# Attention logits with the head indicator stationary and the products streaming through four 32-column tiles

## The chip, the cores and the metric

The kernel runs on one core of a Trainium2 chip. The metric is the device time of one execution in microseconds (us). In the profile PE is TensorE (its matmuls), PEld its weight loads, DVE is VectorE, ACT is ScalarE, POOL is GpSimd.

## The reference

One transformer block over 2048 positions of width 576: a modulated layer norm, local attention with 32 heads of 18 channels, a projection, a second modulated layer norm, and a gated MLP with 4608 hidden channels. The change touches the logits of the attention alone. Each position looks at eight keys, at distances 0, 2, ... 14:

```python
idx = pos[:, None] - off[None, :]            # off = 0, 2, ..., 14
kg = k[:, :, idx_c, :].reshape(B, H, S, W, Dh)      # W = 8, Dh = 18
logits = jnp.einsum('bhsd,bhswd->bhsw', q, kg) * scale
logits = jnp.where(mask[None, None, :, :], logits, -1000000000.0)
attn = _softmax(logits, axis=-1)
```

## The kernel before

The sequence is cut into 8 chunks of 256 positions. Three pieces of work run per chunk: `stage_a` (layer norm, the q, k and v projections `pq` and `pv`), `stage_b` (logits, softmax, weighted sum of V, output projection `pw`, second layer norm) and `mlp` (matmuls `pgu`, `acc`, `accr`). `stage_a` and `stage_b` of later chunks are generators that the MLP loop advances one `yield` at a time, so that their matmuls mix with those of the MLP. Before the first MLP there is a start-up in which `stage_b(0)` and `stage_a(1)` alternate.

The logits before: for each of the eight key offsets, DVE multiplies q by the shifted k (`prod`, channels on the partitions). TensorE then sums each head's 18 channels, with `prod` as the stationary operand and a 0/1 head indicator `ind` of 32 columns streaming.

```python
lnp   = tile_pool(name="lnp", bufs=2)    # ln_xn
hTp   = tile_pool(name="hTp", bufs=3)    # ln_hT
prodp = tile_pool(name="prodp", bufs=2)
smp   = tile_pool(name="smp", bufs=2)    # dd
# ... (stage_b)
lg = psum_tile([P, ST, W, H], F32, name="lg")
for i in range(W):
    off = HALO - DIL * (W - 1 - i)
    prod = prodp.tile([P, KT, CH], BF, name="prod")
    nc.vector.tensor_tensor(prod[:], qT[:], kT[:, :, off:off + CH], ALU.mult)
    with hp():
        for j in range(ST):                # two halves of 128 positions
            for m in range(KT):            # five slices of 128 channels
                nc.tensor.matmul(lg[:, j, i, :], lhsT=prod[:, m, j * P:(j + 1) * P], rhs=ind[:, m, :],
                                 start=(m == 0), stop=(m == KT - 1))
    if i % 2 == 1:
        yield
# ... softmax over lg: maskneg (chunk 0 alone), mx, dd, ssum, attn

def interleave(g1, g2):                    # advances stage_b and stage_a in turn
    gs = [g for g in (g1, g2) if g is not None]
    while gs:
        for g in list(gs):
            try:
                next(g)
                yield
            # ...
```

Of the kernel before, what the change touches and what calls it, by code (L numbers as in the profile page):

```python
# [7 lines left out]
BF = mybir.dt.bfloat16  # L8
F32 = mybir.dt.float32
ALU = mybir.AluOpType  # L10
# [5 lines left out]
P = 128  # L16
D = 576
DP = 640
KT = 5
H = 32  # L20
DH = 18
W = 8
DIL = 2
FF = 4608
FT = FF // P
HALO = 16
EPS = 1e-5
NEG = -1.0e9
CH = 256
ST = CH // P  # L30
# [26 lines left out]
def kernel(  # L57
# [14 lines left out]
    nc = tc.nc  # L72
# [6 lines left out]
    def hp():  # L79
        return tc.high_priority() if cfg["hi_pe"] else nullcontext()  # L80
# [2 lines left out]
    wts = ctx.enter_context(tc.tile_pool(name="wts", bufs=1))  # L83
    dramp = ctx.enter_context(tc.tile_pool(name="dramp", bufs=1, space=DRAM))
    xin = ctx.enter_context(tc.tile_pool(name="xin", bufs=6))
    lnp = ctx.enter_context(tc.tile_pool(name="lnp", bufs=2))
    small = ctx.enter_context(tc.tile_pool(name="small", bufs=2))
    hTp = ctx.enter_context(tc.tile_pool(name="hTp", bufs=3))
    qkp = ctx.enter_context(tc.tile_pool(name="qkp", bufs=2))
    vstage = ctx.enter_context(tc.tile_pool(name="vstage", bufs=2))  # L90
    prodp = ctx.enter_context(tc.tile_pool(name="prodp", bufs=2))
    smp = ctx.enter_context(tc.tile_pool(name="smp", bufs=2))
    attnp = ctx.enter_context(tc.tile_pool(name="attnp", bufs=2))
    vshp = ctx.enter_context(tc.tile_pool(name="vshp", bufs=2))
    ps_att = ctx.enter_context(tc.tile_pool(name="ps_att", bufs=3, space=PSUM))
# [7 lines left out]
    def psum_tile(shape, dt, name):  # L103
        return ps_att.tile(shape, dt, name=name, tag="att")

    ident = consts.tile([P, P], BF, name="ident")
# [3 lines left out]
    ind = consts.tile([P, KT, H], BF, name="ind")  # L110
# [252 lines left out]
    def stage_b(ci):  # L363
        s0 = ci * CH
        cd = chunk[ci]
        x_t, qT, kT = cd["x_t"], cd["qT"], cd["kT"]
        vshs = []
        for j in range(ST):
# [2 lines left out]
            src = bass.AP(vd.tensor, vd.offset + base * D, [[D, P], [DIL * D, W], [1, D]])  # L371
            dma_vsh.dma_start(vsh[:].rearrange("p w d h -> p w (d h)"), src)
            vshs.append(vsh)
        lg = psum_tile([P, ST, W, H], F32, name="lg")
        for i in range(W):
            off = HALO - DIL * (W - 1 - i)
            prod = prodp.tile([P, KT, CH], BF, name="prod")
            nc.vector.tensor_tensor(prod[:], qT[:], kT[:, :, off:off + CH], ALU.mult)  # L378
            with hp():
                for j in range(ST):  # L380
                    for m in range(KT):
                        nc.tensor.matmul(lg[:, j, i, :], lhsT=prod[:, m, j * P:(j + 1) * P], rhs=ind[:, m, :],  # L382
                                         start=(m == 0), stop=(m == KT - 1))
            if i % 2 == 1:
                yield
        mx = small.tile([P, ST, H], F32, name="mx")
        dd = smp.tile([P, ST, W, H], F32, name="dd")
        if ci == 0:
# [42 lines left out]
        for j in range(ST):  # L431
            pw = psum_tile([P, 512], F32, name="pw")
            with hp():
                for m in range(KT):
                    nc.tensor.matmul(pw[:], lhsT=oT[:, m, j * P:(j + 1) * P], rhs=wo[:, m, 0:512],  # L435
                                     start=(m == 0), stop=(m == KT - 1))
                for m in range(KT):
                    nc.tensor.matmul(pwr[:, j, :], lhsT=oT[:, m, j * P:(j + 1) * P], rhs=wo[:, m, 512:D],
                                     start=(m == 0 and j == 0), stop=(m == KT - 1), skip_group_check=True)
# [93 lines left out]

    run(stage_a(0))
    run(interleave(stage_b(0), stage_a(1) if NCH > 1 else None))
    for ci in range(NCH):
        gb_ = stage_b(ci + 1) if ci + 1 < NCH else None
        ga_ = stage_a(ci + 2) if ci + 2 < NCH else None
        bg = interleave(gb_, ga_)
        mlp(ci, bg)  # L540
        run(bg)
# [30 lines left out]
```

## Time and profile before

| | before |
|---|---|
| time, median of 4 runs | 650.53 us (649.53 to 653.12) |
| PE busy | 92% of the span |
| PE busy from 45 to 75 us | 21.4 of 30 us, clock 0.76 |
| first MLP matmul | 68.8 us |
| end of the first MLP | 160.0 us |
| one chunk after that | 75.0 us |

From the page of the kernel before, busy time per engine, and two rows of the 40 slices (tenths busy; granted clock in tenths):

```profile
PE 597.5 (92%) x5700; PEld 450.0 (70%) x5788; DVE 319.9 (49%) x733; ACT 277.0 (43%) x518; POOL 141.1 (22%) x221
...
PE   2766999999999999999999999999999999999996
...
PEclk9979799999999999999999999999999999999999
```

TensorE is full from the fifth slice on. Only the first 70 us or so have room. Busy time in two stretches, in the order PE, PEld, DVE, ACT, POOL, then clock, DMA share and GB/s, first for the end of the start-up, then for one chunk:

```profile
45.00:75.00 30.00, 21.38 (x215) 14.55 (x217) 22.23 (x43) 13.28 (x28) 6.91 (x14) 0.76 0.83 255
```
```profile
310.03:385.05 75.02, 72.97 (x696) 55.12 (x706) 38.80 (x90) 34.13 (x64) 16.52 (x26) 1.00 0.38 116
```

The waits of PE in that chunk (who waited for whom, us in total, times, longest) come to 1.3 us:

```profile
PE oT_pA L425 <- DVE o_sb L416: 0.7, 1, 0.7
PE ln_pA L287 <- ACT ln_xn L278: 0.4, 1, 0.4
PE lg L382 <- DVE prod L378: 0.2, 1, 0.2
```

The group of the logit matmuls (count, busy us, mean ns of one, idle before):

```profile
L382 PE MATMUL lg<-ind,prod 128*128 128x32 bf16 x640 | 32.4, 180 | 2.3 <-DVE prod L378 2.1
```

The 180 ns is the length of one record, not what one matmul costs. The PE timeline of the kernel before, in which neighbours of one group are merged (start us, length us, count at the end), shows the pace:

```profile
319.53 0.22 PE L287 MATMUL ln_pB<-ident,ln_xn 128*128 128x128 bf16 x1
319.58 0.66 PE L382 MATMUL lg<-ind,prod 128*128 128x32 bf16 x20
320.09 0.19 PE L471 MATMUL accr<-wd_blk,hh 128*128 128x64 bf16 x1
...
321.17 0.18 PE L382 MATMUL lg<-ind,prod 128*128 128x32 bf16 x1
321.19 0.22 PE L287 MATMUL ln_pA<-ident,ln_xn 128*128 128x128 bf16 x1
321.25 0.18 PE L382 MATMUL lg<-ind,prod 128*128 128x32 bf16 x1
```

Twenty logit matmuls take 0.51 us from 319.58 to the next start at 320.09: 25 ns each, and 80 of them 2.0 us a chunk. This is the floor for small matmuls that the Trainium skill gives ("TensorE: Matmul & The Clock Gate", "Back-to-back issue gap": about 25 ns for 1 to 64 columns). At the 109 ns that 256 columns take here, 32 columns alone would need about 14 ns (an estimate), so a form with longer streams could save at most some 1 us of 75 us. The last lines show that logit matmuls and layer norm transposes alternate freely, at no cost.

### The profile page before, as it was taken

To read this page: it belongs to the slowest core of one execution; us is meant where nothing else is said; L and a number is where in the kernel's file an instruction comes from. 1 tells how busy PE (TensorE), PEld (TensorE's weight loads), DVE (VectorE), ACT (ScalarE), POOL (GpSimd) and SP (SyncE) were. 2 spreads that over 40 slices of the span, in tenths; PEclk is the share of its full clock that TensorE was granted. 3 is DMA by queue.
4 is the path that set the end of the run, shared out by engine and by line. 5 is a ranking of instruction groups with operands and counts; after the bars stand their busy time and mean duration, and the time that the engine had idled before them with its cause. 6 is when DMAs were issued, how large, how long until landed. Compare 5 with 4: busy or idle time off the path is not lost.

```text
span 647.4 us, 13700 instructions
## 1 busy us (share of the span) xinstructions
PE 597.5 (92%) x5700; PEld 450.0 (70%) x5788; DVE 319.9 (49%) x733; ACT 277.0 (43%) x518; POOL 141.1 (22%) x221
## 2 busy tenths in 40 slices
PE   2766999999999999999999999999999999999996
PEld 1543767677767777677776777677776777777774
DVE  5387788712891158611893138811594152113112
ACT  2523646433653337433563337433443335333332
POOL 7014021222112221322212221112211222222220
PEclk9979799999999999999999999999999999999999
DMA  8699658693326341533406332353322333333331
GB/s 254 173 315 286 195 181 257 204 284 101 95 60 216 97 127 55 189 105 92 129 29 230 92 104 69 113 175 93 110 74 57 96 110 89 92 96 111 97 99 41
DMA packets 41094, 87.24 MB, mean 135 GB/s; under 512 B 4857, under 2 KB 27721, under 8 KB 41033
## 3 DMA queue, kind: packets, MB, share of 16 engines
q0 software_dynamic: 15872, 61.35, 31.7%
q1 hardware_dynamic: 22857, 22.66, 11.9%
q10 hardware_dynamic: 2304, 2.36, 1.1%
q8 instruction: 45, 0.74, 0.5%
q14 instruction: 16, 0.13, 0.1%
HBM read 81.62 MB, written 5.40 MB: 134 GB/s over the span
## 4 chain that ended last, share of the span: by engine, by line
PE 63%; DVE 22%; ACT 7%; DMA 4%; issue 1%; SPq 1%; POOL 0%; ACTq 0%
PE pgu L482 30%; PE pgu L484 8%; DVE vsh L412 5%; PE accr L471 4%; PE pw L435 3%; DVE vsh L414 3%; DVE ln_stats L267 2%; ACT ln_xn L278 2%; ACT ln_hT L296 2%; DMA wgu<-in_B_w_up_dram 2%; PE ln_pA L287 1%; PE lg L382 1%; DVE hh L494 1%; ACT gu L493 1%; PE acc_8289 L469 1%
## 5 line engine op out<-in xcount | busy, mean ns | idle before, releaser
L482 PE MATMUL pgu<-ln_hT,wgu 128*128 128x256 bf16 x2304 | 337.2, 273 | 0.0
L493 ACT CAST gu<-pgu 128x512 bf16<-128x512 f32 x288 | 168.6, 586 | 263.4 <-PE pgu L484 263.2
L482 PEld LDWEIGHTS <-wgu 128*128 128x128 bf16 x2304 | 205.5, 98 | 50.8 <-issue 1.2
L494 DVE TENSOR_TENSOR hh<-gu 128x256 bf16<-128x256 bf16 x288 | 83.5, 291 | 284.5 <-ACT gu L493 284.1
L477 POOL DMA_DIRECT2D wd_blk<-in_B_w_down_dram x144 | 102.5, 712 | 343.3 <-PE accr L471 337.8
L471 PE MATMUL accr<-wd_blk,hh 128*128 128x64 bf16 x576 | 110.9, 193 | 3.8
L469 PEld LDWEIGHTS <-hh 128*128 128x128 bf16 x576 | 56.3, 98 | 40.9 <-DVE hh L494 4.1
L484 PE MATMUL pgu<-ln_hT,wgur 128*128 128x256 bf16 x288 | 78.6, 273 | 0.0
L484 PE MATMUL pgu<-ln_hTu,wgur 128*128 128x256 bf16 x288 | 78.5, 272 | 0.0
L336 PE MATMUL pq<-ln_hT,wqk 128*128 128x256 bf16 x400 | 56.9, 279 | 8.1 <-ACT ln_hT L296 6.3
L484 PEld LDWEIGHTS <-wgur 128*128 128x128 bf16 x576 | 56.4, 98 | 6.3
L471 PEld LDWEIGHTS <-hh 128*128 128x128 bf16 x576 | 56.2, 98 | 3.0
L378 DVE TENSOR_TENSOR prod<-qT,kT 128x1280 bf16<-128x1280 bf16 x64 | 51.1, 821 | 12.9 <-ACT kT L341 9.9
L336 PEld LDWEIGHTS <-wqk 128*128 128x128 bf16 x400 | 38.4, 100 | 16.4 <-issue 7.0
L412 DVE TENSOR_TENSOR vsh<-vsh,attn 128x4608 bf16<-128x4608 bf16 x16 | 40.3, 2555 | 0.2
L382 PE MATMUL lg<-ind,prod 128*128 128x32 bf16 x640 | 32.4, 180 | 2.3 <-DVE prod L378 2.1
L382 PEld LDWEIGHTS <-prod 128*128 128x128 bf16 x640 | 26.9, 98 | 9.9 <-DVE prod L378 7.5
L296 ACT ACTIVATE ln_hT<-ln_pA,modc 128x256 bf16<-128x256 bf16 x32 | 18.1, 564 | 18.0 <-PE ln_pA L287 8.3
L287 PE MATMUL ln_pA<-ident,ln_xn 128*128 128x128 bf16 x128 | 16.5, 232 | 8.7 <-ACT ln_xn L278 7.9
L287 PEld LDWEIGHTS <-ln_xn 128*128 128x128 bf16 x160 | 13.2, 103 | 15.0 <-ACT ln_xn L278 13.5
L351 PE MATMUL pv<-wv,ln_hT 128*128 128x512 bf16 x72 | 21.0, 378 | 1.0 <-ACT kT L341 0.5
L414 DVE TENSOR_TENSOR vsh<-vsh 128x2304 bf16<-128x2304 bf16 x16 | 21.4, 1369 | 0.0
(218 smaller groups left out, 581.7 us busy)
## 6 DMA issues: line engine op xcount, KB each, us to landing
wd_blk<-in_B_w_down_dram POOLq DMA_DIRECT2D x144, 288.0 KB, 3.3
vsh<-vd POOLq DMA_DIRECT2D x16, 1152.0 KB, 7.4
wgu<-in_B_w_gate_dram SPq DMA_DIRECT2D x9, 512.0 KB, 6.7
wgu<-in_B_w_up_dram SPq DMA_DIRECT2D x9, 512.0 KB, 7.6
wm<-in_w_mod_dram SPq DMA_DIRECT2D x6, 576.0 KB, 5.6
x_t<-in_A_x_dram SPq DMA_DIRECT2D x16, 144.0 KB, 2.8
vd<-v_sb ACTq DMA_DIRECT2D x16, 144.0 KB, 1.8
out_dram<-o_t SPq DMA_DIRECT2D x16, 144.0 KB, 3.1
```

The source lines that it names most:

```text
L336: nc.tensor.matmul(pq[:, gi, :], lhsT=wqk[:, kt, t, m * P:(m + 1) * P], rhs=hT[:, kt, :], start=(kt == 0), stop=(kt == KT - 1))
L378: nc.vector.tensor_tensor(prod[:], qT[:], kT[:, :, off:off + CH], ALU.mult)
L382: nc.tensor.matmul(lg[:, j, i, :], lhsT=prod[:, m, j * P:(j + 1) * P], rhs=ind[:, m, :], start=(m == 0), stop=(m == KT - 1))
L412: nc.vector.tensor_tensor(vsh[:], vsh[:], attn[:, j, :, None, :].to_broadcast([P, W, DH, H]), ALU.mult)
L414: ge.tensor_tensor(vsh[:, 0:4], vsh[:, 0:4], vsh[:, 4:8], ALU.add)
L469: nc.tensor.matmul(acc[j][:], lhsT=hh[:, j * P:(j + 1) * P], rhs=wd_blk[:, f % WDB, 0:512], start=(f == 0), stop=(f == FT - 1))
L471: nc.tensor.matmul(accr[:, j, :], lhsT=hh[:, j * P:(j + 1) * P], rhs=wd_blk[:, f % WDB, 512:D], start=(f == 0 and j == 0), stop=(f == FT - ...
L477: dma_wd.dma_start(wd_blk[:], B_w_down[f * P:(f + WDB) * P, :].rearrange("(k p) n -> p k n", p=P))
L482: nc.tensor.matmul(pgu[:, t, :], lhsT=wgu[:, kt, t, f * P:(f + 1) * P], rhs=h2T[:, kt, :], start=(kt == 0), stop=False)
L484: nc.tensor.matmul(pgu[:, t, :], lhsT=wgur[:, f * P:(f + 1) * P], rhs=(h2T[:, KT - 1, :] if t == 0 else h2Tu[:]), start=False, stop=True)
L493: nc.scalar.copy(gu[:], pgu[:])
L494: hh_inst = nc.vector.tensor_tensor(hh[:], gu[:, 0, :], gu[:, 1, :], ALU.mult)
```

## The change

The operands swap roles: the indicator (32 columns) becomes stationary and the product streams, 256 positions at once. A 32-column weight has a quarter of the usual 128 columns, so four key offsets go to four column tiles (a quarter of the array's columns each), whose outputs land on PSUM partitions 0, 32, 64 and 96. The result has heads and offsets on the partitions, so ACT evicts it as bf16 and four transposes bring positions back to the partitions. A group needs four products at a time: `prod` gets five buffers, and three other pools shrink to make room.

```diff
-    lnp = ctx.enter_context(tc.tile_pool(name="lnp", bufs=2))
+    lnp = ctx.enter_context(tc.tile_pool(name="lnp", bufs=1))
-    hTp = ctx.enter_context(tc.tile_pool(name="hTp", bufs=3))
+    hTp = ctx.enter_context(tc.tile_pool(name="hTp", bufs=2))
-    prodp = ctx.enter_context(tc.tile_pool(name="prodp", bufs=2))
-    smp = ctx.enter_context(tc.tile_pool(name="smp", bufs=2))
+    prodp = ctx.enter_context(tc.tile_pool(name="prodp", bufs=5))
+    smp = ctx.enter_context(tc.tile_pool(name="smp", bufs=1))
# ... the loop of the old form goes, and in its place:
+        WG = W // 2
+        lgT = psum_tile([P, 2, CH], F32, name="lgT")
+        for g in range(2):
+            prods = []
+            for i in range(g * WG, (g + 1) * WG):
+                off = HALO - DIL * (W - 1 - i)
+                prod = prodp.tile([P, KT, CH], BF, name="prod")
+                nc.vector.tensor_tensor(prod[:], qT[:], kT[:, :, off:off + CH], ALU.mult)
+                prods.append(prod)
+                if i % 2 == 1:
+                    yield
             with hp():
+                for m in range(KT):
+                    for wi in range(WG):
+                        nc.tensor.matmul(lgT[wi * H:(wi + 1) * H, g, :], lhsT=ind[:, m, :], rhs=prods[wi][:, m, :],
+                                         start=(m == 0), stop=(m == KT - 1), skip_group_check=True)
+            yield
+        lgs = smp.tile([P, 2, CH], BF, name="lgs")
+        nc.scalar.copy(lgs[:], lgT[:])
+        lg = psum_tile([P, ST, W, H], BF, name="lg")
+        with hp():
+            for j in range(ST):
+                for g in range(2):
+                    nc.tensor.transpose(lg[:, j, g * WG:(g + 1) * WG, :].rearrange("p w h -> p (w h)"),
+                                        lgs[:, g, j * P:(j + 1) * P], ident[:])
+        yield
```

More of the change, by code (lines that the diff above doesn't have):

```diff
@@ L373, in stage_b @@
             vshs.append(vsh)
-        lg = psum_tile([P, ST, W, H], F32, name="lg")
-        for i in range(W):
-            off = HALO - DIL * (W - 1 - i)
-            prod = prodp.tile([P, KT, CH], BF, name="prod")
-            nc.vector.tensor_tensor(prod[:], qT[:], kT[:, :, off:off + CH], ALU.mult)
-            with hp():
-                for j in range(ST):
-                    for m in range(KT):
-                        nc.tensor.matmul(lg[:, j, i, :], lhsT=prod[:, m, j * P:(j + 1) * P], rhs=ind[:, m, :],
-                                         start=(m == 0), stop=(m == KT - 1))
-            if i % 2 == 1:
-                yield
+        WG = W // 2
[9 more added lines that the diff above has]
+                    yield
+            with hp():
+                for m in range(KT):
[12 more added lines that the diff above has]
+        yield
         mx = small.tile([P, ST, H], F32, name="mx")
```

## The prediction

> **What bounds the kernel now.** TensorE. The page's busy table has PE 92%, DVE 49%, ACT 43%. Between 145 and 425 us the table by stretches has PE at 68.0 of every 70 us, clock 1.00, and one chunk lasts 75.0 us (the `o_t` evictions in the chain of waits stand at 235.0, 310.0, 385.1). In the PE timeline matmuls follow each other at stream pace: 109 ns per 256-column matmul, 216 ns per 512-column one. The waits of PE for anybody in the chunk 310 to 385 sum to only 1.3 us. So time moves only with TensorE's stream time per chunk, or with the first 75 us, where PE is busy for 45 us and latency counts.
>
> **What is removed.** 80 matmuls per chunk `lg<-ind,prod` (128x32), 640 in all. The groups list shows 32.4 us busy, 180 ns each, but that overlaps: in the PE timeline 20 of them start within 0.50 us, so 25 ns each. Their true cost is 2.0 us per chunk, 16 us in all, plus about 0.3 us of waits for `prod` per chunk.
>
> **What is added, per chunk.**
> - 40 matmuls of 256 columns, weights of 32 columns. One after the other they would cost 40 x 109 ns = 4.4 us. If four 32-column tiles stream at once (the Trainium skill, "TensorEngine Tiling (Array Packing)", Key Properties, says that tiles operate independently; no run here shows it yet), 10 x about 115 ns = 1.15 us. I expect mostly overlap: 1.2 to 1.5 us.
> - 4 transposes, about 56 ns each in the timeline: 0.22 us.
> - Mode switches. The same section says that a change of tiling mode drains the array. A matmul's record outlasts its own 13 ns stream by about 160 ns, so I estimate 0.15 us a switch. At least four per chunk (0.6 us). The order of `lg` and `ln_pA` before alternates one by one at 321 and 326 us; if the new matmuls get interleaved with full-width ones like that, 8 to 12 switches (1.2 to 1.8 us).
> - ACT: one 128x512 eviction, 0.59 us (as `gu`). ACT has room. DVE reads bf16 logits: no change expected. `prod` stays 0.82 us x8, but with five buffers no longer waits for PE.
>
> **Sum.** Before 2.0 + 0.3 us; after 1.3 + 0.22 + 0.6 to 1.5 us. Per chunk -0.2 to +0.7 us, in all -2 to +6 us.
>
> **Other parts.** In the start-up, the longer way from `prod` to softmax (eviction 0.6 us, transposes, two handovers) adds about 1 us for chunk 0. One buffer for `ln_xn`, two for `ln_hT`: an `hT` for a later chunk must wait until the running MLP has read its `hT`; background work moves later, into the next MLP, but PE has matmuls to fill with, so I expect little (0 to +2 us). The `x1` buffers already hold background work back to the end of each MLP (`x1` follows `o_t` directly at 311.9 us).
>
> **Prediction.** 652 us; 643 to 672 us should hold it 8 times in 10. Faster by over 2%: 0.04; within 2%: 0.77; slower by over 2%: 0.19.
>
> **What would show the steps.** Right: `lgT` matmuls start about 25 to 35 ns apart in the PE timeline, in blocks of 20; gaps of 0.1 to 0.2 us at each border between `lgT` and full-width matmuls; the chunk stays within 1 us of 75.0; PE waits stay small.
>
> **What would make it wrong.** If `lgT` matmuls start 109 ns apart, the tiles don't overlap, and the time is about 670 us. If switches cost nothing, about 645 us. If PE waits for `ln_hT` or the `att` PSUM buffers near MLP borders, the smaller pools cost more than I think, and the first 75 us or the `o_t` spacing will show it.

## More of the kernel before

The build fixes the order of each engine's instructions ahead of time. It starts from the order in the program, lets `hp()` (high priority) come forward, and passes over what it believes is not ready. Where a `yield` stands therefore decides what comes first.

## The result

The changed kernel takes 668.32 us (median of 4 runs, 665.76 to 668.65), against 650.53 us before. The ratio is 1.0265, 95% interval 1.0237 to 1.0293: slower by 2.7%.

| | before | after |
|---|---|---|
| time | 650.53 us | 668.32 us |
| logit matmuls | 640 of 32 columns | 320 of 256 columns, 32 transposes |
| PE busy from 45 to 75 us | 21.4 us | 13.8 us |
| chunk 0's softmax starts | 37.5 us | 44.9 us |
| first MLP matmul | 68.8 us | 77.2 us |
| end of the first MLP | 160.0 us | 160.7 us |
| one chunk after that | 75.0 us | 76.3 us |
| longer chunk in which the last background work lands | none | 79.5 us |

Both end the first MLP at nearly the same time, but the kernel before had by then done more: 200 of 400 `pq` matmuls, against 154. The deferred work lands later.

From the page after, busy time and the group of the new matmuls:

```profile
PE 611.4 (92%) x5500; PEld 443.6 (67%) x5500; DVE 319.6 (48%) x733; ACT 279.9 (42%) x526; POOL 145.1 (22%) x221
...
L388 PE MATMUL lgT<-prod,ind 128*32 128x256 bf16 x320 | 21.5, 287 | 0.8 <-DVE prod L381 0.8
```

The PE timeline after, one chunk's logits in the steady part:

```profile
351.46 0.61 PE L388 MATMUL lgT<-prod,ind 128*32 128x256 bf16 x13
352.00 0.56 PE L287 MATMUL ln_pA<-ident,ln_xn 128*128 128x128 bf16 x7
352.40 0.22 PE L287 MATMUL ln_pB<-ident,ln_xn 128*128 128x128 bf16 x1
352.55 0.40 PE L388 MATMUL lgT<-prod,ind 128*32 128x256 bf16 x8
...
353.77 0.27 PE L388 MATMUL lgT<-prod,ind 128*32 128x256 bf16 x1
353.98 0.50 PE L496 MATMUL pgu<-ln_hT,wgu 128*128 128x256 bf16 x3
...
354.73 0.28 PE L388 MATMUL lgT<-prod,ind 128*32 128x256 bf16 x1
...
355.87 0.72 PE L388 MATMUL lgT<-prod,ind 128*32 128x256 bf16 x17
356.52 0.61 PE L496 MATMUL pgu<-ln_hT,wgu 128*128 128x256 bf16 x4
```

Three things can be read here. First, the tiles do overlap: 17 matmuls take 0.65 us, where 17 in a row at 109 ns would take 1.85 us. In the single records four start 3 to 4 ns apart, and the next four 109 ns after the first. The Trainium skill says the same ("TensorE: Matmul & The Clock Gate", "Part 3: Packing small matmuls": about 4 ns between the starts of tiles). Second, a lone matmul occupies a whole slot: 0.21 us from 353.77 to 353.98, the 109 ns of a slot and the price of leaving that comes next. Third, each border between full-width and 32-column matmuls has a price. Over 100 to 560 us, the first `lgT` of a block starts 93 ns later than the pace allows (24 borders, 5% to 95%: 93 to 94 ns). A full-width matmul starts 205 ns after the last `lgT` (30 borders, median), 96 ns more than one 109 ns slot. The block structure 13, 8, 1, 1, 17 has ten borders a chunk. What the price consists of is not shown: in the PEld records the weight load of the first full-width matmul also starts only at 353.97 us, within 0.01 us of its matmul, where inside a block it starts a slot ahead. A drain of the array and a weight load that nothing hides (its record lasts 0.1 us) are not told apart by any run here.

The sum per chunk, from starts to next starts on PE (all 640 and all 320 logit matmuls are in the traces, though a few other matmul records are missing): after, `lgT` 1.95 us including the exits, 0.54 us lost at the entries, transposes 0.22 us, together 2.7 us. Before, 2.04 us plus 0.68 us lost in front of logit matmuls, also 2.7 us. **On TensorE in the steady part the new form costs what the old one did.** That does not explain 18 us.

The same two stretches and the waits after:

```profile
45.00:75.00 30.00, 13.79 (x138) 7.66 (x135) 23.79 (x45) 6.67 (x16) 5.91 (x12) 0.73 0.85 268
```
```profile
313.30:389.60 76.30, 74.01 (x672) 54.23 (x671) 38.88 (x89) 34.38 (x66) 17.88 (x25) 1.00 0.38 113
```
```profile
PE ln_pA L287 <- ACT ln_xn L278: 1.1, 2, 0.7
PE acc_3992 L483 <- DVE hh L508: 0.6, 1, 0.6
PE oT_pA L439 <- DVE o_sb L430: 0.4, 2, 0.2
```

The start-up stands out. The PE timeline after, where chunk 0's second group of logits should come:

```profile
37.14 0.40 PE L388 MATMUL lgT<-prod,ind 128*32 128x256 bf16 x1
37.47 1.30 PE L336 MATMUL pq<-ln_hT,wqk 128*128 128x256 bf16 x6
38.69 0.28 PE L388 MATMUL lgT<-prod,ind 128*32 128x256 bf16 x1
38.91 0.61 PE L336 MATMUL pq<-ln_hT,wqk 128*128 128x256 bf16 x4
39.45 0.51 PE L388 MATMUL lgT<-prod,ind 128*32 128x256 bf16 x10
40.08 2.39 PE L336 MATMUL pq<-ln_hT,wqk 128*128 128x256 bf16 x20
42.41 0.40 PE L388 MATMUL lgT<-prod,ind 128*32 128x256 bf16 x7
44.09 0.23 PE L397 MATMUL lg<-ident,lgs 128*128 128x128 bf16 x1 [1.28 <-ACT lgs L392]
```

DVE had the last of chunk 0's eight products ready at 37.3 us. PE nevertheless works through chunk 1's `pq` in between, and finishes chunk 0's logits only at about 42.8 us. The DVE timeline (in brackets: idle before, and who ended it), first of the kernel before, then after:

```profile
37.50 0.42 DVE L389 TENSOR_TENSOR dd<-lg,maskneg 128x256 f32<-128x256 f32 x1 [0.51 <-PE lg L382]
```
```profile
44.85 0.42 DVE L403 TENSOR_TENSOR dd<-lg,maskneg 128x256 f32<-128x256 bf16 x1 [7.59 <-PE lg L397]
...
46.61 0.81 DVE L381 TENSOR_TENSOR prod<-qT,kT 128x1280 bf16<-128x1280 bf16 x1
...
48.02 0.82 DVE L381 TENSOR_TENSOR prod<-qT,kT 128x1280 bf16<-128x1280 bf16 x1
...
50.42 0.81 DVE L381 TENSOR_TENSOR prod<-qT,kT 128x1280 bf16<-128x1280 bf16 x1
...
51.75 0.82 DVE L381 TENSOR_TENSOR prod<-qT,kT 128x1280 bf16<-128x1280 bf16 x1
```

DVE sits idle for 7.59 us, the softmax starts 7.4 us later, and four products of chunk 1 stand inside it. PE then waits for the result of this chain, the weighted sum `o_sb`, which it transposes; first before, then after:

```profile
54.86 0.39 PE L425 MATMUL oT_pA<-ident,o_sb 128*128 128x128 bf16 x4
```
```profile
61.81 0.29 PE L439 MATMUL oT_pA<-ident,o_sb 128*128 128x128 bf16 x1 [9.18 <-DVE o_sb L430]
```

So PE is busy for 7.6 us less between 45 and 75 us. The chain that ended last (the view `--critical`: start us, length us) shows that these logits came onto it only with the change. Before, it goes through weight transfers in this stretch; after, through chunk 1's `pq` in front of chunk 0's logits:

```profile
36.07 13.36 DMA wgu<-in_B_w_up_dram
49.45 4.96 DMA wgur<-in_B_w_gate_dram
```
```profile
40.08 2.30 PE pq L336 x19
```

### The profile page after: what moved, and what is told of

It is laid out like the page before. It is cut to its first block, busy times and chain, and to the rows that moved or that the text cites. A ratio compares the mean times of both kernels' runs of the same rounds, so it can differ in the third digit from the quotient of the medians.

```text
span 666.9 us, 13200 instructions
## 1 busy us (share of the span) xinstructions
PE 611.4 (92%) x5500; PEld 443.6 (67%) x5500; DVE 319.6 (48%) x733; ACT 279.9 (42%) x526; POOL 145.1 (22%) x221
## 4 chain that ended last, share of the span: by engine, by line
PE 66%; DVE 22%; ACT 8%; issue 2%; DMA 1%; SPq 1%; ACTq 0%; POOL 0%; DVEq 0%; POOLq 0%
PE pgu L496 27%; PE pq L336 7%; PE pgu L498 7%; DVE vsh L426 6%; PE pw L449 3%; DVE vsh L428 3%; PE lgT L388 3%; DVE ln_stats L267 2%; ACT ln_xn L278 2%; DVE hh L508 2%; PE accr L485 2%; ACT gu L507 2%; ACT ln_hT L296 2%; DVE vsh L429 2%; PE ln_pA L287 1%
## 5 line engine op out<-in xcount | busy, mean ns | idle before, releaser
L336 PE MATMUL pq<-ln_hT,wqk 128*128 128x256 bf16 x400 | 60.6, 286 | 6.3 <-ACT ln_hT L296 5.5
L287 PE MATMUL ln_pA<-ident,ln_xn 128*128 128x128 bf16 x128 | 14.2, 238 | 13.2 <-ACT ln_xn L278 12.9
L287 PEld LDWEIGHTS <-ln_xn 128*128 128x128 bf16 x160 | 10.6, 105 | 22.5 <-ACT ln_xn L278 20.2
L328 POOL COPY kT<-kT 128x80 bf16<-128x80 bf16 x7 | 10.2, 1458 | 68.1 <-ACT kT L341 68.1
L372 POOL DMA_DIRECT2D vsh<-vd x16 | 14.5, 908 | 38.0 <-DVE o_sb L430 29.9
L388 PE MATMUL lgT<-prod,ind 128*32 128x256 bf16 x320 | 21.5, 287 | 0.8 <-DVE prod L381 0.8
L449 PE MATMUL pw<-wo,oT 128*128 128x512 bf16 x80 | 21.0, 411 | 1.2 <-ACT oT L440 1.0
```

The lines of the kernel that those rows point to most:

```text
L336: nc.tensor.matmul(pq[:, gi, :], lhsT=wqk[:, kt, t, m * P:(m + 1) * P], rhs=hT[:, kt, :], start=(kt == 0), stop=(kt == KT - 1))
L388: nc.tensor.matmul(lgT[wi * H:(wi + 1) * H, g, :], lhsT=ind[:, m, :], rhs=prods[wi][:, m, :], start=(m == 0), stop=(m == KT - 1), skip_gro ...
L449: nc.tensor.matmul(pw[:], lhsT=oT[:, m, j * P:(j + 1) * P], rhs=wo[:, m, 0:512], start=(m == 0), stop=(m == KT - 1))
```

## The experiments

Two theories from this reading, and a third from the size of the pools:

- **P**: the smaller pools push background work out of the start-up and make PE wait.
- **S**: the switches between 32-column and full-width matmuls cost the time.
- **O**: the order costs it. In the new form a group's matmuls stand in the program after two `yield`s, so chunk 1's projections get in front of chunk 0's logits, through which the changed kernel's longest chain of the start-up runs.

All twelve runs gave correct results.

### The pools alone, in the old form

```diff
 # in the kernel before
-lnp bufs=2, hTp bufs=3, smp bufs=2
+lnp bufs=1, hTp bufs=2, smp bufs=1
```

> The kernel before with only the three smaller pools of the change (one buffer of ln_xn, two of ln_hT, one of dd), prod still in two buffers, logits in the old form. Theory P (the pools cost the time: stage work of a later chunk is pushed out of the start-up, PE waits more for ln_xn): 660 to 668 us, the last background work lands in a longer stretch after 460 us, and PE waits for ln_xn rise to about 12 us. Theory O (the order of the start-up with the new form costs it: chunk 0's softmax begins 7.4 us later because its logit matmuls stand behind chunk 1's projections and prod steps stand in its softmax): 649 to 655 us, chunk 0's softmax still begins near 37.5 us.

Measured: 649.92 us, ratio 0.9996 (0.9973 to 1.0019): no difference. The softmax of chunk 0 starts at 38.8 us, 1.3 us later than before.

```diff
 # and, in the next run, also
-prodp bufs=2
+prodp bufs=5
```

> The kernel before with all four pool sizes of the change, prod in five buffers too, logits in the old form. Theory P: 660 to 668 us as with three pools. Theory O: 650 to 656 us, as the old matmuls can follow each prod at once; at most prod steps of chunk 1 moved into chunk 0's softmax cost 2 to 3 us.

Measured: 645.48 us, ratio 0.9932 (0.9910 to 0.9954): 0.7% faster, not slower, and below both expected ranges. The softmax of chunk 0 starts where it did in the kernel before:

```profile
37.46 0.42 DVE L389 TENSOR_TENSOR dd<-lg,maskneg 128x256 f32<-128x256 f32 x1 [0.64 <-PE lg L382]
```

Theory P falls for the old form. Background work of a later chunk does move out of the start-up (154 of 400 `pq` by the end of the first MLP, and a chunk of 77.1 us near the end), but the first MLP then ends earlier, at 147.1 us, and the sum is the same. Five `prod` buffers are worth about 4 us against two (ratio 0.9932 against 0.9996). So the fair comparison for the new form is this kernel, with the same four pool sizes: against it the change costs 3.3 points of the ratio (1.0265 against 0.9932), about 22 us, not 18.

Where they go in the two profiled executions (spans 643.3 and 666.9 us), from the first `o_t` eviction of each chunk:

| | first MLP ends | next four chunks | chunk after them | rest, to the last MLP's end |
|---|---|---|---|---|
| old form, all four pools | 147.1 us | 297.8 us (74.4 each) | 77.1 us | 115.8 us |
| changed kernel | 160.7 us | 305.2 us (76.3 each) | 79.5 us | 116.1 us |
| difference | +13.6 | +7.4 | +2.4 | +0.3 |

### The pools given back, in the new form

```diff
 # in the changed kernel
-lnp bufs=1, hTp bufs=2, prodp bufs=5
+lnp bufs=2, hTp bufs=3, prodp bufs=4
-gb_bc, ga_bc: F32
+gb_bc, ga_bc: BF
-wv_raw = sp.tile([P, KT, D], BF, name="wv_raw")
+wv_raw = vshp.tile([P, W, DH, H], BF, name="vsh").rearrange(...)[...]   # for room
```

> The changed kernel with two buffers of ln_xn and three of ln_hT again, prod in four buffers, one dd; room for it from loading the raw V weights into a vsh buffer and keeping the two gate rows in bf16 (rounding of the gates changes slightly). Theory P: back to 649 to 655 us. Theory O: 660 to 668 us, first MLP matmul still near 77 us.

Measured: 679.42 us, ratio 1.0461 (1.0430 to 1.0493): slower still, outside both expectations. The trace shows 12 blocks of `lgT` a chunk instead of 5, 3.24 us in them plus 1.46 us lost at entries, and 78.0 us a chunk. The next run asks whether four `prod` buffers did that.

```diff
-prodp bufs=5
+prodp bufs=4
```

> The changed kernel with four prod buffers instead of five and nothing else. Six blocks per chunk instead of five (13, 7, 1, 1, 1, 17), chunk 0 in 15 blocks instead of 8. If the fourth-buffer limit was what made the run with the larger ln pools slow (679 us), this is near 675 to 680 us; if it was the other order that larger ln pools bring (12 blocks a chunk), this is 668 to 673 us.

Measured: 669.23 us, ratio 1.0287 (1.0262 to 1.0312), 6 blocks, 76.6 us a chunk: about the changed kernel's own time. So it was not the fourth buffer alone. It came with the other order of PE's instructions that the larger layer norm pools (or the two edits made for room, which were not run alone) brought. With 12 blocks, `lgT` and its entries take 2.2 us a chunk more than in the changed kernel, while the chunk is 1.7 us longer: switches do cost when there are many.

### The overlap of the tiles, taken away in part

```diff
-                for m in range(KT):
-                    for wi in range(WG):
+                for wi in range(WG):
+                    for m in range(KT):
```

> The changed kernel with the two inner loops swapped, so that the five matmuls of one column tile follow each other and neighbours in the stream mostly use the same tile. If the 109 ns per four that the trace shows is overlap between tiles, they now start 109 ns apart, 4.4 us per chunk instead of about 1.4 us: +2.5 to +3 us per chunk, 685 to 695 us in all. If overlap is an artefact of how the records are modelled, the time stays near 668 us.

Measured: 678.22 us, ratio 1.0442 (1.0417 to 1.0467), 78.1 us a chunk, with 3.63 us in `lgT` instead of 1.95 us. The direction is the expected one and the size is smaller. Neighbours in the stream still fall on different tiles where one tile's five end and the next begin: the 40 matmuls of a chunk took 26 slots, not 40 (13 in the changed kernel). The overlap is real. Losing half of it cost 1.7 us a chunk in `lgT`, of which the exits of two more blocks (7 instead of 5) are about 0.2 us.

### The order: the inner yields removed

```diff
                 prods.append(prod)
-                if i % 2 == 1:
-                    yield
```

> The changed kernel without the yields between the prod steps of a group, so that the 20 logit matmuls of a group come in the program ahead of chunk 1's projections. In the instruction order of PE chunk 0's last logit matmul moves from place 229 to 189. Theory O (start-up order): chunk 0's softmax begins 3 to 5 us earlier than at 44.9 us and the whole takes 660 to 665 us. Rival S (the switches between full-width and 32-column matmuls cost the time, wherever they are): 666 to 670 us, since the blocks per chunk hardly change.

Measured: 655.26 us, ratio 1.0083 (1.0060 to 1.0107). Two lines that compute nothing give back about two thirds of the loss against the kernel before (1.8 of 2.65 points of the ratio, about 12 us), or a bit over half of the 3.3 points against the old form with the same pools: more than expected. The softmax of chunk 0 starts 5.9 us earlier than in the changed kernel, with no product of chunk 1 inside it:

```profile
39.00 0.42 DVE L401 TENSOR_TENSOR dd<-lg,maskneg 128x256 f32<-128x256 bf16 x1 [2.03 <-PE lg L395]
```

The first MLP ends at 155.2 us (5.5 us earlier), and a chunk takes 74.7 us instead of 76.3. The blocks per chunk hardly change (4 instead of 5). Of the 1.6 us gained in a steady chunk, `lgT` and its entries give 0.3 us and PE's waits 1.2 us, so the gain is mostly not switches. PE's waits in one chunk (cf. the three lines of the changed kernel, 2.1 us) are now:

```profile
PE ln_pA L287 <- ACT ln_xn L278: 0.5, 1, 0.5
PE acc L481 <- DVE hh L506: 0.4, 1, 0.4
```

Theory O holds for the 5.5 us that came back by the end of the first MLP, and order accounts for most of the steady 1.9 us too. Which displaced instruction makes `ln_pA` and `acc` wait was not isolated. What this kernel still loses against the old form with these pools is 8.1 us by the end of the first MLP. There `lgT` of chunks 0 and 1 takes 6.03 and 5.22 us, in 3 and 16 blocks, waits for products and a lower clock included (granted 0.78 from 45 to 75 us), against 3.19 and 2.81 us for `lg`, counted the same way. Chunk 0's softmax no longer decides it: in this run the chain that ended last goes through a transfer of MLP weights again (10.8 us from 42.47 us), and the softmax starts only 1.5 us later than in the old form with these pools.

A control for the old form (all four pools of the change, yielding after every fourth offset):

```diff
-            if i % 2 == 1:
+            if i % 4 == 3:
                 yield
```

> Control: the old logits with all four pool sizes of the change, yielding after every fourth offset instead of every second, as the changed kernel without inner yields does. If the 13 us gained there came from the yields alone, for any form, this gains too or shows how much mere reordering moves the old form: I expect within 3 us of the 645.5 us with the usual yields, since the old matmuls follow each prod either way.

Measured: 648.79 us, ratio 0.9959 (0.9940 to 0.9979), within the expected 3 us if 0.9959 is set against 0.9932. In the old form the yields are worth little in the whole time, and in the other direction. But in the start-up the sparser yields cost the old form too: its first MLP ends at 151.4 us instead of 147.1 us. So of the 8.1 us above, 4.3 us appear without the new form, and 3.8 us are left for the form itself: its chunk 1 takes 5.22 us in `lgT`, against 2.84 us in `lg` here. A steady chunk takes 74.3 us here, against 74.7 us. Mere reordering moves the old form by some 2 us, so differences of that size between two kernels here say nothing about their form.

### The old form in the start-up, the new one after it

```diff
+        if ci < 2:
+            lg = psum_tile([P, ST, W, H], F32, name="lg")
+            # the old loop
+        else:
+            # the new form
```

> Chunks 0 and 1 with the old logits, chunks 2 to 7 with the new form, pools as in the change. Theory O: the first MLP ends near 148 us as in the old form with these pools (147.1), then 76.3 us per chunk as in the changed kernel: 654 to 658 us. Theory S: only 2 of 8 chunks are relieved, 662 to 666 us.

Measured: 654.96 us, ratio 1.0081 (1.0054 to 1.0107). The first MLP ends at 146.2 us, then come chunks of 76.3 us. This separates the two parts: with the old logits in chunks 0 and 1 the whole start-up loss is gone and the whole steady loss remains. Six of eight chunks still switch as before, so theory S, which expected 662 to 666 us, does not carry the start-up loss. This run alone does not say how much of that loss is order and how much is the new logits' own time in these two chunks: the run without inner yields gives 5.5 of the 13.6 us to the order, and the control suggests a further 4.3 us that come with the sparser yields that remain.

### Fewer switches

```diff
-                    for wi in range(WG):
+                    for wi in (WG - 1, *range(WG - 1)):
```

The matmuls of a group keep their order on PE; with the last product's tile first, none starts alone.

> The changed kernel with the column tile whose prod comes last put first, so that no logit matmul of a group can start before all four prods are there. In the order of PE a chunk's logit matmuls then stand in 3 blocks (14, 6, 20) instead of 5 (13, 8, 1, 1, 17) from chunk 2 on, and in 6 instead of 8 for chunk 0. From the trace a switch costs about 95 ns on each side, and a lone matmul a whole 109 ns slot: 0.7 to 0.9 us less per chunk. Theory S: 660 to 663 us. Theory O alone: 664 to 668 us, as chunk 0's logits still end at place 229.

Measured: 663.96 us, ratio 1.0215 (1.0192 to 1.0239), just below the range for O alone and just above that for S. Three blocks a chunk, `lgT` 1.54 instead of 1.95 us, 75.8 us a chunk instead of 76.3. Each chunk gains 0.5 us, less than the expected 0.7 to 0.9 us: `lgT` lost 0.41 us, but the entries only 0.09 us, as one of the three now costs 0.26 us instead of 0.09 us. Switches cost time, and they are the small part.

> As the run before it (old logits in chunks 0 and 1), with the last prod's tile first in the others: 3 blocks instead of 5. The two theories together: 0.8 us less per chunk than without, 649 to 653 us; it would still not beat the old form with the same pools (645.5 us) unless the new form were worth something at 3 blocks.

Measured: 652.22 us, ratio 1.0039 (1.0013 to 1.0065). The two edits add up: 75.8 us a chunk after a first MLP that ends at 145.4 us.

Next, no inner yields and the last tile first, in all chunks:

> The changed kernel in all chunks, without inner yields and with the last prod's tile first. Two blocks of 20 in chunks 3 to 6, but chunks 0 and 1 cut into 10 and 16 blocks: from 655.3 us of the one edit, less about 0.6 us a chunk in five chunks: 650 to 654 us.

Measured: 656.78 us, ratio 1.0088 (1.0067 to 1.0108): no better than the yields alone, against the expectation. The steady chunk is a little shorter (74.6 us, two blocks), but the first MLP ends 3.2 us later (158.4 us), with chunk 0's logits in 10 blocks and its softmax at 44.3 us.

Last, the candidate: old form in chunks 0 and 1, then the new form with both edits.

> The candidate: old logits in chunks 0 and 1, new form without inner yields and with the last prod's tile first in chunks 2 to 7, pools as in the change. In the order of PE chunks 3 to 6 have two blocks of 20. Theory: start-up as in the old form with these pools (first MLP ends near 146 us), lgT about 1.35 us a chunk with four switches, 74.0 to 74.6 us a chunk: 641 to 646 us. If the new form with the fewest switches were worth its 0.5 us a chunk, it beats the old form with these pools (0.9932 of before) by up to 3 us; otherwise it ties.

Measured: 646.56 us, ratio 0.9928 (0.9907 to 0.9948), just above the expected range: 0.7% faster than the kernel before, well below the changed kernel, and level with the old form with the same pools (0.9932). Its PE timeline shows the two blocks:

```profile
318.22 0.73 PE L400 MATMUL lgT<-prod,ind 128*32 128x256 bf16 x20
318.88 0.39 PE L508 MATMUL pgu<-ln_hT,wgu 128*128 128x256 bf16 x2
...
321.71 0.73 PE L400 MATMUL lgT<-prod,ind 128*32 128x256 bf16 x20
322.38 0.28 PE L508 MATMUL pgu<-ln_hT,wgu 128*128 128x256 bf16 x1
```

In this best order the new logits cost 1.32 us including exits, 0.31 us at the entries and 0.23 us for transposes, 1.9 us a chunk, against 2.4 us for the old form with the same pools (2.02 us plus 0.38 us lost before them). The chunk still takes 74.6 us against 74.4, since PE waits longer elsewhere (1.1 us for `ln_xn` against 0.5). The tiling's own gain is at most half a microsecond in 75 and does not come through in the time.

## Why the prediction was right or wrong

The stated range, 643 to 672 us, holds the 668.3 us. The centre, 652 us, was 16 us too low, and the likeliest class, "within 2%" at 0.77, was not what came. That the range holds the time is partly luck: the prediction named tiles that don't overlap and smaller pools as what could make it slow, and neither did.

- *"What bounds the kernel now. TensorE."* Right. The PE stays full after the start-up in both kernels.
- *"I expect mostly overlap: 1.2 to 1.5 us."* Right: four starts within about 10 ns, 109 ns per four. Measured 1.95 us with the exits of five blocks in it, so about 1.5 us without. The sign named for it, starts 25 to 35 ns apart, was the average and not the pattern.
- *"I estimate 0.15 us a switch."* Mis-sized: 0.093 us going in and 0.096 us coming out. The count, "8 to 12", was right at ten. In sum the term of 0.6 to 1.5 us measured about 1.0 us.
- *"Per chunk -0.2 to +0.7 us."* Right for the logits themselves (about 0 against before). But "the chunk stays within 1 us of 75.0" failed: 76.3 us. Removing two `yield`s brought it to 74.7 us, so most of that is order, which the prediction did not cost.
- *"In the start-up, the longer way from `prod` to softmax ... adds about 1 us for chunk 0."* This is the step that failed. The softmax started 7.4 us later, PE stood 9.2 us for the weighted sum that follows it, and the first MLP matmul came 8.4 us later. The prediction added up durations along the chain (eviction, transposes, handovers) and took the place of the matmuls in PE's order as given. The changed order put chunk 1's projections in front of them. The softmax is not all of it: without the inner yields it starts at 39.0 us, and the first MLP matmul still comes only at 75.0 us.
- *"Background work moves later ... but PE has matmuls to fill with, so I expect little (0 to +2 us)."* Right for the pools: 0.0% for three of them, and 0.7% faster with five `prod` buffers. Filling works in the steady part; in the start-up there was nothing to fill with, which the PE row between 45 and 75 us shows.

## What to carry to other kernels

Where one engine is full except in the start-up, cost a change twice: by its work in the steady part, and by where its instructions come in each engine's order in the start-up, where a chain that was not the longest can become it. A form that collects several inputs before it issues anything moves its matmuls past the next yield point, and other work slips in front; removing two lines of yields gave back about two thirds of the loss against the kernel before. And compare a new form with the old one at the new buffer counts, since here the buffers alone made the old form 0.7% faster and hid part of the loss.

## What the Trainium skill lacked or had wrong

- "TensorEngine Tiling (Array Packing)", Key Properties, says that a change of tiling mode drains the array, but gives no cost. Here it was 93 ns going from full width to 32 columns and 96 ns coming back, per border (the drain itself was not measured apart from the weight load there), and with 5 blocks a chunk it took back the tiles' gain.
- The same page, "When to Use Tiling", recommends the swap of stationary and streaming operand with 4x column tiling for a 32-column streaming side. Here the most that could be had was 2.0 us to 1.1 us a chunk (80 x 25 ns against 10 x 109 ns), because the old form already sat at the 25 ns floor rather than at a full slot; with switches and the transposes back it was 2.4 to 1.9 us at best. The page does not name the transposes back as a cost.
- "TensorE: Matmul & The Clock Gate", Part 3, says that matmuls run in strict order, but no page names the order itself as a cost when one matmul that heads a long chain stands behind others that do not matter yet. Here removing two lines of `yield`s was worth about 12 us of 668.
